# Mamba2 scan feeding a SiLU MLP on one core: how the first unit's C, its decay masks and the opening of the matrix engine are ordered

## The chip, the core and the metric

The kernel runs on one core of a Trainium2 chip. The metric is the device time of one execution in microseconds (us). Seven runs of the kernel before gave a median of 350.6 us, from 350.04 to 353.39.

The core's engines work side by side, each through its own queue of instructions in order: TensorE (PE) multiplies matrices out of SBUF into PSUM, VectorE (DVE), ScalarE (ACT) and GpSimd (POOL) work element by element, SyncE (SP) and ACT issue transfers (DMAs). An instruction that waits holds up all that is queued behind it on its engine.

## What is computed

The input is a state space scan with 4 batches, 8 heads, 768 time steps, 32 channels per head and a state of 16, and an MLP of 256 to 2048 to 256 behind it, all in float32:

```python
L  = exp(cum[:, None] - cum[None, :]) * causal   # decay from step j to step i, in a chunk
y  = ((C @ B.T) * L) @ x  +  (C @ state) * exp(cum)
state = exp(sum(log a)) * state + sum_j decay_from_j * B_j x_j
h  = y_of_all_heads @ w_in
out = (h * sigmoid(h)) @ w_out
```

## The kernel before

The time axis is cut into 12 units of 256 steps (three to a batch), each into four chunks of 64. For a unit, E holds the decays L, G is C times B for each head, M is E times G (written over E), Y the two products that give the scan's output, XM its copy in SBUF. Then come `f_s1` (times w_in, then SiLU) and the product with w_out. Later pairs of units use a seven-product scheme that saves one product in eight; the change does not touch it.

The order of instructions on every engine is written out by hand: the program's order is the engines' order. The text that matters is the opening, until the matrix engine has a backlog of `f_s1` pieces.

**Loads.** SP issues in this order: the first rows of `a` (L192, into `ach`), C of unit 0 in four pieces (`load_t`, L115), `a` again spread over partitions (`pa01`, L200), x of unit 0 (L122), three pieces of w_in (`raw`, L156), B, C and x of unit 1, more weights. ACT issues B of unit 0 (`bn`, L107) and nothing else. `load_unit` calls the same `load_t` for the first unit of each later batch, on SP.

**E of unit 0.** `f_A` (L215) clips the rows of `a`, on DVE. `f_Ab` (L309) spreads them over 128 partitions with one float32 matmul of 512 columns into a PSUM tile `hp` (three buffers), which the machine runs as two passes. `scan_E` (L300, instruction at L304) turns it into E by a scan over 512 columns. There are two such spreads and two scans for a unit, k = 0 and 1.

**C of unit 0.** `f_T(0, 1)` (L347) transposes it on DVE into CT; `f_T2` (L367) makes two masked copies CE on ACT, with `par` (L264) as the mask: two small DVE reductions over `hm`, which POOL makes (L257 to L260).

**B of unit 0.** `f_TP` (L351) transposes it on PE, ACT copies it out (L359), `f_G0` (L406) multiplies it with CE. `f_B` (POOL, L341) multiplies B with the last column of E, and `f_D0` (L391) multiplies that with x; `f_S` (DVE, L430 and L432) makes the chunk states from it, with the decays that `f_P01` (L277, L280) makes from `pa01`. `f_SM` (L440) copies them, `f_M` (L417) makes M, `f_Y` (L460, L469) Y and `f_X` (L482) XM.

**Weights.** Each w_in piece is unpacked on ACT (`w_size`, L164 and L168), DVE (`w_bits`, L176 to L180) and POOL (L184).

**Fillers.** `busy(n, small)` (L223) issues matmuls on zeros: n of 512 bfloat16 columns, then `small` of 64. Their operand `idle` is cleared by a memset (L221) first. Their output goes to the single buffer of `o_ps`.

The part of the order that the change edits, before:

```python
    f_T(0, 1)
    for e in range(2):
        f_T2(0, e)
    f_Ab(0, 0)
    f_Ab(0, 1)
    f_TP(0)
    busy(0, 18)
    f_G0(0)
    busy(2, 10)
    f_Ek(0, 0)
    f_Ek(0, 1)
```

Of the kernel before, what the change touches and what calls it, by code (L numbers as in the profile page):

```python
# [8 lines left out]
FP32 = mybir.dt.float32  # L9
# [3 lines left out]
ALU = mybir.AluOpType  # L13
AX = mybir.AxisListType
# [7 lines left out]
def kernel(  # L22
# [22 lines left out]
    nc = tc.nc  # L45

    batch, H, S, D = x.shape
    N = B.shape[-1]
    Q = 64
# [21 lines left out]
    ps_h = ctx.enter_context(tc.tile_pool(name="ps_h", bufs=3, space=bass.MemoryType.PSUM))  # L71
    ps_o = ctx.enter_context(tc.tile_pool(name="ps_o", bufs=1, space=bass.MemoryType.PSUM))
# [4 lines left out]
    pa, ab, bn, tbc, xt = ({} for _ in range(5))  # L77

    def at(u):
        return u // UPB, u % UPB * UT  # L80

    def load_pa(u, q):

        b, t0 = at(u)
        pa[u] = loads.tile([128, UT], FP32, name="pa")
        q.dma_start(out=pa[u], in_=bass.AP(tensor=a.tensor, offset=a.offset + b * H * S + t0,
                                           ap=[[S, H], [0, N], [1, UT]]))

    def load_ab(u, q):

        b, t0 = at(u)
        ab[u] = loads2.tile([128, 2, H, Q], FP32, name="ab")
        for t in range(4):
            k, c = divmod(t, 2)
            q.dma_start(out=ab[u][64 * c:64 * c + 64, k],
                        in_=bass.AP(tensor=a.tensor, offset=a.offset + b * H * S + t0 + t * Q,
                                    ap=[[0, 64], [S, H], [1, Q]]))

    def load_n(u, i, q):

        b, t0 = at(u)
        if i == 0:
            t = bn[u] = loads.tile([128, 2, H, N], FP32, name="bn")
        else:
            t = tbc[u] = loads.tile([128, 2, 2, 8, N], FP32, name="tbc")[:, 0]
        for k in range(2):
            q.dma_start(out=t[:, k], in_=(B, C)[i][b, :, t0 + 128 * k:t0 + 128 * k + 128].rearrange("h p n -> p h n"))  # L107

    def load_t(u, i, q):

        b, t0 = at(u)
        if u not in tbc:
            tbc[u] = loads.tile([128, 2, 2, 8, N], FP32, name="tbc")
        for g in range(4):
            q.dma_start(out=tbc[u][32 * g:32 * g + 32, i],  # L115
                        in_=(B, C)[i][b, 2 * g:2 * g + 2, t0:t0 + UT].rearrange("e (t r) n -> t e r n", r=8))

    def load_x(u, q):
        b, t0 = at(u)
        xt[u] = loads.tile([128, 2, H, D], FP32, name="xt")  # L120
        for k in range(2):
            q.dma_start(out=xt[u][:, k], in_=x[b, :, t0 + 128 * k:t0 + 128 * k + 128].rearrange("h p d -> p h d"))  # L122

    def load_unit(u):
        load_pa(u, nc.sync)
        if 0 < u < UPB:
            load_n(u, 1, nc.sync)
        else:
            load_t(u, 0, nc.sync)
            load_t(u, 1, nc.sync)  # L130
        load_n(u, 0, nc.sync)
        load_ab(u, nc.sync)
        load_x(u, nc.sync)
# [26 lines left out]
    def w_size(n, what="uv"):  # L160
        if n in raw:
            if "u" in what:
                u = wu[n] = wtp.tile([128, 2, WF], FP32, name="wu")
                nc.scalar.activation(u, raw[n][:, :, :, 1].bitcast(FP32), AF.Abs)  # L164
            if "v" in what:
                v = wv[n] = wtp.tile([128, 2, WF], FP32, name="wv")

                nc.scalar.activation(v, raw[n][:, :, :, 0], AF.Copy, scale=2.0 ** -51, bias=2.0)  # L168
# [20 lines left out]
    A0, A1 = 96, 96 + S // Q  # L189
    early = gpool.tile([128, NF, UT], FP32, name="gT")  # L190
    ach = early[:, 0:2].rearrange("p a (h t) -> p (a h) t", t=Q)
# [3 lines left out]
    QZ = 8 * (Q + 1)  # L195
    pa01 = flat[:, 6 * UT:8 * UT]
    pz01, one01, pfx01 = (flat[:, 8 * UT + QZ * i:8 * UT + QZ * (i + 1)] for i in range(3))
    load_t(0, 1, nc.sync)
    load_n(0, 0, nc.scalar)
    nc.sync.dma_start(out=pa01, in_=bass.AP(tensor=a.tensor, offset=a.offset, ap=[[S, H], [0, N], [1, 2 * UT]]))  # L200
    load_x(0, nc.sync)
# [13 lines left out]
    def f_A():  # L215
        nc.vector.tensor_scalar(out=ach[A0:A1], in0=ach[A0:A1], scalar1=1.0, scalar2=1e-6, op0=ALU.min, op1=ALU.max)
        nc.vector.memset(ach[A0:A1, :, 0:1], 0.0)


    idle = early[:, 4].bitcast(BF16)  # L220
    nc.vector.memset(idle, 0.0)  # L221

    def busy(n, small=0):  # L223
        t = ps_o.tile([128, 512], FP32, name="o_ps")
        for i in range(n):
            nc.tensor.matmul(out=t, lhsT=idle[:, 0:128], rhs=idle, start=True, stop=True)  # L226
        for i in range(small):
            nc.tensor.matmul(out=t[:64, :64], lhsT=idle[:, 0:64], rhs=idle[:, 64:128], start=True, stop=True)  # L228
# [3 lines left out]
    sel = early[:, 2:4].rearrange("p a (s c t) -> p (a s) c t", s=2, c=2)  # L232
# [11 lines left out]
                                fill=1.0, base=-64 * c, channel_multiplier=1)  # L244
    tiny = const.tile([128, 1], FP32, name="tiny")
    nc.scalar.activation(tiny, idle[:, 0:1], AF.Silu)
    busy(5)
    f_A()
    ident = const.tile([128, 128], FP32, name="ident")
    nc.vector.memset(ident, 0.0)  # L250
# [5 lines left out]
    hm = const.tile([128, H], FP32, name="hm")  # L256
# [3 lines left out]
    nc.gpsimd.affine_select(out=hm, in_=hm, pattern=[[N, H]], compare_op=ALU.is_ge,  # L260
                            fill=0.0, base=N - 1, channel_multiplier=-1)
    par = const.tile([128, 2], FP32, name="par")
    for e in range(2):
        nc.vector.tensor_reduce(out=par[:, e:e + 1], in_=hm[:, e::2], op=ALU.add, axis=AX.X)  # L264

    pz = const.tile([128, 4, Q + 1], FP32, name="pz")
    one = const.tile([128, 4, Q + 1], FP32, name="one")
# [32 lines left out]
    def scan_E(u, g0, n, t):  # L300

        if g0 == 0:
            E[u] = sc.tile([128, 2, H, Q], FP32, name="E")
        nc.vector.tensor_tensor_scan(out=E[u].rearrange("p k h t -> p (k h t)")[:, Q * g0:Q * (g0 + n)],  # L304
                                     data0=t.rearrange("p g t -> p (g t)"),
                                     data1=diag[:, 0:n].rearrange("p g t -> p (g t)"),
                                     initial=0.0, op0=ALU.mult, op1=ALU.add)

    def f_Ab(u, k):  # L309

        ab[u, k] = t = ps_h.tile([128, H, Q], FP32, name="hp")
        nc.tensor.matmul(out=t.rearrange("p h t -> p (h t)"),  # L312
                         lhsT=sel[:A1, 2 * u + k].rearrange("r c m -> r (c m)"),
                         rhs=ach[:A1].rearrange("r h t -> r (h t)"), start=True, stop=True)

    def f_Ek(u, k):
        scan_E(u, H * k, H, ab.pop((u, k)))

    def f_E0(u, i, n):

# [23 lines left out]
    def f_T(u, i):  # L344

        t = (BH, CT)[i][u] = sc.tile([128, UT], FP32, name=("bh", "ct")[i])
        nc.vector.transpose(out=t.rearrange("p (t r) -> p r t", r=8), in_=tbc[u][:, i].rearrange("p e r n -> p r e n"))  # L347
        if i == 1:
            tbc.pop(u)

    def f_TP(u):  # L351

        tp = ps_o.tile([128, 512], FP32, name="o_ps")
        for i, t in enumerate((bn[u],) if u == 0 else (bn[u], tbc.pop(u))):
            for k in range(2):
                nc.tensor.transpose(out=tp[:, 256 * i + 128 * k:256 * i + 128 * k + 128],  # L356
                                    in_=t[:, k].rearrange("p h n -> p (h n)"), identity=ident)
        BH[u] = sc.tile([128, UT], FP32, name="bh")
        nc.scalar.activation(BH[u], tp[:, 0:256], AF.Copy)  # L359
        if u > 0:  # L360
            CT[u] = tp[:, 256:512]

    def f_T2(u, e):

        if e == 0:
            CE[u] = sc.tile([128, 2, UT], FP32, name="ce")
        nc.scalar.activation(CE[u][:, e], CT[u], AF.Copy, scale=par[:, e:e + 1])  # L367
# [29 lines left out]
    def f_G0(u):  # L397

        bh, ce = BH.pop(u), CE[u]
        if u not in DP:  # L400
            DP[u] = ps_s.tile([128, 4, 512], FP32, name="gy")
        for k in range(2):
            for c in range(2):
                ts = slice(128 * k + 64 * c, 128 * k + 64 * c + 64)
                for g in range(4):
                    nc.tensor.matmul(out=DP[u][64 * c:64 * c + 64, g, 128 * k:128 * k + 128],  # L406
                                     lhsT=bh[32 * g:32 * g + 32, ts], rhs=ce[32 * g:32 * g + 32, :, ts],
                                     start=True, stop=True, tile_position=(32 * g, 64 * c), skip_group_check=True)
# [401 lines left out]


    f_T(0, 1)
    for e in range(2):
        f_T2(0, e)
    f_Ab(0, 0)
    f_Ab(0, 1)
    f_TP(0)
    busy(0, 18)
    f_G0(0)
    busy(2, 10)  # L820
    f_Ek(0, 0)
    f_Ek(0, 1)
    f_B(0)
    f_D0(0, True)
# [6 lines left out]
    w_size(0)  # L831
    w_bits(0, 2)
    f_Ab(1, 0)
    w_size(1)
    busy(3, 18)
    f_Y(0)

    f_Ek(1, 0)
    f_Ab(1, 1)
    f_X(0)  # L840
    w_size(2)
    w_bits(1, 2)
    load_unit(2)
    f_s1(0, 0)
    f_TP(1)
# [34 lines left out]
    for g, j, todo in steps:  # L880
        f_s1(g, j)
        w_steps(todo)
    load_unit(3)
    late = ("b13 s14", "b14 s15", "b15")

# [122 lines left out]
```

## Time and profile before

| what | value |
|---|---|
| median of seven runs | 350.6 us (350.04 to 353.39) |
| the profiled execution's own time | 350.04 us |
| its span | 348.3 us, so 1.74 us lie around the span |
| TensorE busy | 342.3 us, 98% of the span |
| VectorE, ScalarE, GpSimd busy | 203.9, 162.6, 112.0 us |
| first matmul of `f_s1` | 14.68 us into the span |
| the stretch from which `f_s1` runs without a stop | from 24.50 us |

A row of the timeline gives the start in us from the span's beginning, the duration in us, engine, line, operation, the tile written and the tile read, the shape and the count of like instructions merged into the row; in square brackets stands the idle time before it and what ended that. SPq and ACTq are the issuing of transfers. Busy time of TensorE includes the fillers, so a full row of TensorE says little about the opening. The chain of waits is read backwards from the last instruction: each row is what released the next one.

### The profile page before, as it was taken

The page shows a single profiled execution, that of the slowest core. Times are in us where ns is not written, and L with a number is a line of the kernel's source. Part 1 is how long each engine was busy: PE and PEld are TensorE (multiplying, and loading weights), DVE is VectorE, ACT ScalarE, POOL GpSimd, SP SyncE. Part 2 cuts the span into 40 slices and gives each one's busy share as a digit, 9 for nine tenths or more (in the row PEclk, how much of TensorE's full clock was granted, in tenths as well). Part 3 has the DMA queues.
Part 4 walks back from the last instruction along what each step waited for, and adds up shares of the span by engine and source line. Part 5 has one row for each costly group of instructions (what it writes and reads, how often), then busy time and mean ns, then how long its engine had stood idle before and what let it go on. Part 6 is the DMA issues. An engine that isn't in the chain of part 4 may idle for free.

```text
span 348.3 us, 8381 instructions
## 1 busy us (share of the span) xinstructions
PE 342.3 (98%) x3323; PEld 288.4 (83%) x3324; DVE 203.9 (59%) x406; ACT 162.6 (47%) x399; POOL 112.0 (32%) x140
## 2 busy tenths in 40 slices
PE   8999999999999999999999999999999999999996
PEld 3678888888888888888888888888888888888886
DVE  7998799975795665543763563664652231233912
ACT  3677394323323545455545454644545454454010
POOL 4355345444285122244042244042234112041200
PEclk9999999999999999999999999999999999999999
DMA  6977997699857698857189947057504237512202
GB/s 120 213 216 194 224 334 131 120 210 215 142 111 126 121 187 149 162 107 133 23 166 165 172 91 115 16 102 142 94 2 75 44 56 143 107 24 53 41 7 46
DMA packets 117056, 42.66 MB, mean 122 GB/s; under 512 B 102424, under 2 KB 108824, under 8 KB 117016
## 3 DMA queue, kind: packets, MB, share of 16 engines
q1 hardware_dynamic: 110472, 25.73, 36.2%
q0 software_dynamic: 4464, 16.25, 25.0%
q8 instruction: 26, 0.43, 0.5%
q10 hardware_dynamic: 2080, 0.13, 0.4%
q14 instruction: 14, 0.11, 0.1%
HBM read 22.70 MB, written 3.15 MB: 74 GB/s over the span
## 4 chain that ended last, share of the span: by engine, by line
PE 97%; DVE 1%; ACT 1%; issue 0%; POOL 0%; DVEq 0%; ACTq 0%
PE o_ps L648 36%; PE hp L703 29%; PE hp L505 16%; PE hp L648 3%; PE gy L469 3%; PE gy L460 2%; PE o_ps L611 2%; PE gy L406 2%; PE hp L312 1%; PE gy L391 1%; PE hp L626 1%; PE o_ps L226 1%; PE o_ps L356 0%; PE o_ps L228 0%; DVE E L417 0%
## 5 line engine op out<-in xcount | busy, mean ns | idle before, releaser
L706 DVE TENSOR_TENSOR gT<-hp,p 128x256 f32<-128x256 f32 x64 | 26.8, 419 | 73.6 <-ACT p L717 37.6
L648 PE MATMUL o_ps<-gT,w_out_sb 128*128 128x256 f32 x240 | 60.4, 380 | 0.0
L709 ACT ACTIVATE gT<-gT 128x256 f32<-128x256 f32 x96 | 39.7, 414 | 43.9 <-DVE gT L706 43.9
L505 PE MATMUL hp<-XM,w_in_sb 128*128 128x256 f32 x256 | 59.3, 382 | 0.8 <-ACT XM L482 0.5
L505 PEld LDWEIGHTS hp<-XM,w_in_sb 128*128 128x128 f32 x256 | 48.0, 190 | 8.5 <-POOL w_in_sb L184 1.2
L703 PE MATMUL hp<-raw 128*128 128x256 f32 x192 | 52.7, 380 | 0.0
L558 POOL TENSOR_TENSOR ps<-ps 128x256 f32<-128x256 f32 x35 | 29.5, 843 | 71.2 <-ACT ps L588 69.9
L648 PEld LDWEIGHTS o_ps<-gT,w_out_sb 128*128 128x128 f32 x240 | 45.5, 190 | 6.3
L553 POOL DMA_DIRECT2D gT<-gT x31 | 27.2, 910 | 67.4 <-DVE TN L544 21.5
L703 PEld LDWEIGHTS hp<-raw 128*128 128x128 f32 x192 | 36.2, 190 | 5.4 <-POOL ps L558 0.6
L717 ACT ACTIVATE p<-hp 128x256 f32<-128x256 f32 x64 | 24.5, 383 | 27.4 <-PE hp L703 25.9
L706 DVE TENSOR_TENSOR gT<-hp,u 128x256 f32<-128x256 f32 x32 | 13.6, 424 | 38.6 <-PE hp L703 38.6
L703 PE MATMUL hp<-XM,w_in_sb 128*128 128x256 f32 x128 | 34.1, 389 | 0.0
L507 ACT ACTIVATE gT<-hp 128x512 f32<-128x512 f32 x32 | 18.8, 592 | 25.5 <-PE hp L505 25.5
L703 PEld LDWEIGHTS hp<-XM,w_in_sb 128*128 128x128 f32 x128 | 23.3, 190 | 4.3 <-issue 1.0
L304 DVE TENSOR_TENSOR_SCAN E<-ab,diag 128x256 f32<-128x256 f32 (+1 forms) x32 | 25.1, 825 | 0.8 <-DVE ab L323 0.5
L341 POOL TENSOR_TENSOR BT<-bn,E 128x256 f32<-128x256 f32 x12 | 9.4, 780 | 46.1 <-DVE E L304 38.3
L648 PE MATMUL o_ps<-gT,wu 128*128 128x256 f32 x88 | 22.4, 380 | 0.0
L648 PE MATMUL o_ps<-gT,wv 128*128 128x256 f32 x88 | 22.2, 380 | 0.0
L648 PE MATMUL o_ps<-gT,raw 128*128 128x256 f32 x80 | 20.5, 380 | 0.0
L588 ACT ACTIVATE ps<-o_ps 128x256 f32<-128x256 f32 x35 | 13.3, 382 | 14.8 <-PE o_ps L648 11.8
L703 PE MATMUL hp<-raw,w_in_sb 128*128 128x256 f32 x64 | 19.1, 380 | 0.0
(126 smaller groups left out, 520.4 us busy)
## 6 DMA issues: line engine op xcount, KB each, us to landing
gT<-gT POOLq DMA_DIRECT2D x31, 512.0 KB, 6.1
ab<-in_a_dram SPq DMA_DIRECT2D x40, 128.0 KB
raw<-in_moe_w_in_dram SPq DMA_DIRECT2D x8, 512.0 KB
raw<-in_moe_w_out_dram SPq DMA_DIRECT2D x8, 512.0 KB
xt<-in_x_dram SPq DMA_DIRECT2D x24, 128.0 KB
out_dram<-ot SPq DMA_DIRECT2D x92, 32.0 KB
bn<-in_B_dram SPq DMA_DIRECT2D x22, 64.0 KB
tbc<-in_C_dram SPq DMA_DIRECT2D x40, 32.0 KB
```

Of the source, the lines that this page charges most:

```text
L304: nc.vector.tensor_tensor_scan(out=E[u].rearrange("p k h t -> p (k h t)")[:, Q * g0:Q * (g0 + n)], data0=t.rearrange("p g t -> p (g t)"), ...
L469: nc.tensor.matmul(out=y[32 * q:32 * q + 32, 2 * w + c, 64 * k:64 * k + 64], lhsT=xc[64 * c:64 * c + 64, k, h], rhs=m[64 * c:64 * c + 64, ...
L505: nc.tensor.matmul(out=hp[:, i], lhsT=w_in_sb[:, kc, f * 128:(f + 1) * 128], rhs=xm[:, kc], start=(kc == 0), stop=(kc == KC - 1))
L507: nc.scalar.activation(GTS[g][:, :, j], hp, AF.Silu)
L553: nc.gpsimd.dma_start(out=o[:, js], in_=a[:, js], accum_op=ALU.add)
L558: engine.tensor_tensor(out=o, in0=p, in1=q, op=op)
L588: nc.scalar.activation(p[m].rearrange("p (k c t) -> p c k t", c=2, k=2), o.rearrange("p (c k t) -> p c k t", c=2, k=2), AF.Copy)
L648: nc.tensor.matmul(out=o, lhsT=w(j), rhs=g()[:, j], start=(j == 0), stop=(j == last))
L703: nc.tensor.matmul(out=o, lhsT=w, rhs=x_, start=start, stop=True, skip_group_check=True)
L706: nc.vector.tensor_tensor(out=o, in0=p, in1=q, op=ALU.add)
L709: nc.scalar.activation(o, i, AF.Silu)
L717: nc.scalar.activation(o, i, AF.Copy)
```

## The change

C of unit 0 is loaded on two queues: `load_t` takes two queues and gives its four pieces to them in turn, SP and ACT for unit 0 (SP twice elsewhere). On ACT the two pieces stand ahead of the two of B. DVE transposes C before it makes `par`. The first spread of unit 0 becomes two of 256 columns, each with its own scan; `par` comes behind the first of these scans. The memset of `idle` becomes two, and four matmuls of 128 columns are put ahead of the opening fillers, of which three instead of five are left. The counts of later fillers change.

```diff
-    def load_t(u, i, q):
+    def load_t(u, i, q, q2):
...
-            q.dma_start(out=tbc[u][32 * g:32 * g + 32, i],
+            (q, q2)[g % 2].dma_start(out=tbc[u][32 * g:32 * g + 32, i],
...
-    load_t(0, 1, nc.sync)
+    load_t(0, 1, nc.sync, nc.scalar)
     load_n(0, 0, nc.scalar)
...
-    nc.vector.memset(idle, 0.0)
+    for cs in (slice(0, 128), slice(128, 512)):
+        nc.vector.memset(idle[:, cs], 0.0)
...
-    busy(5)
+    warm = ps_o.tile([128, 512], FP32, name="o_ps")
+    for i in range(4):
+        nc.tensor.matmul(out=warm[:, 0:128], lhsT=idle[:, 0:128], rhs=idle[:, 0:128], start=True, stop=True)
+    busy(3)
     f_A()
...
-    for e in range(2):
-        nc.vector.tensor_reduce(out=par[:, e:e + 1], in_=hm[:, e::2], op=ALU.add, axis=AX.X)
+    def f_par():
+        for e in range(2):
+            nc.vector.tensor_reduce(out=par[:, e:e + 1], in_=hm[:, e::2], op=ALU.add, axis=AX.X)
...
     def f_Ab(u, k):
-        ab[u, k] = t = ps_h.tile([128, H, Q], FP32, name="hp")
-        nc.tensor.matmul(out=t.rearrange("p h t -> p (h t)"),
-                         lhsT=sel[:A1, 2 * u + k].rearrange("r c m -> r (c m)"),
-                         rhs=ach[:A1].rearrange("r h t -> r (h t)"), start=True, stop=True)
-    def f_Ek(u, k):
-        scan_E(u, H * k, H, ab.pop((u, k)))
+        ab[u, k] = []
+        n = H // 2 if u + k == 0 else H
+        for h in range(0, H, n):
+            t = ps_h.tile([128, H, Q], FP32, name="hp")[:, 0:n]
+            ab[u, k].append(t)
+            nc.tensor.matmul(out=t.rearrange("p h t -> p (h t)"),
+                             lhsT=sel[:A1, 2 * u + k].rearrange("r c m -> r (c m)"),
+                             rhs=ach[:A1, h:h + n].rearrange("r h t -> r (h t)"), start=True, stop=True)
+    def f_Ek(u, k, i=0):
+        t = ab[u, k][i]
+        n = t.shape[1]
+        scan_E(u, H * k + n * i, n, t)
...
     f_T(0, 1)
+    f_Ab(0, 0)
+    f_Ek(0, 0)
+    f_par()
     for e in range(2):
         f_T2(0, e)
-    f_Ab(0, 0)
     f_Ab(0, 1)
     f_TP(0)
-    busy(0, 18)
+    busy(0, 14)
     f_G0(0)
-    busy(2, 10)
-    f_Ek(0, 0)
+    busy(2)
+    f_Ek(0, 0, 1)
     f_Ek(0, 1)
...
-    busy(3, 18)
+    busy(3, 28)
     f_Y(0)
```

More of the change, by code (lines that the diff above doesn't have):

```diff
@@ L128, in load_unit @@
         else:
-            load_t(u, 0, nc.sync)
-            load_t(u, 1, nc.sync)
+            load_t(u, 0, nc.sync, nc.sync)
+            load_t(u, 1, nc.sync, nc.sync)
         load_n(u, 0, nc.sync)
```

## The prediction

> **What bounds the kernel now.** I read the page's first and fourth part, then the chain of waits, then the opening's timeline engine by engine.
>
> ```profile
> PE 342.3 (98%) x3323; PEld 288.4 (83%) x3324; DVE 203.9 (59%) x406; ACT 162.6 (47%) x399; POOL 112.0 (32%) x140
> ...
> PE 97%; DVE 1%; ACT 1%; issue 0%; POOL 0%; DVEq 0%; ACTq 0%
> ```
>
> TensorE sets the time, but until 24.50 us much of its work is filler. The change touches the opening alone, so its whole worth is how far it moves this last row of the chain, behind which `f_s1` runs without a stop:
>
> ```profile
> 3.57 2.80 PE hp L312 x4
> ...
> 9.38 0.42 PE hp L391 x32
> 9.80 0.02 issue
> 9.83 0.23 DVE st L430
> ...
> 24.50 12.35 PE hp L505 x56
> ```
>
> The chain passes through the spreads (L312), then `f_D0` (L391), then the states (L430). VectorE's timeline shows who stands beside it:
>
> ```profile
> 3.56 0.43 DVE L255 COPY diag<-gT 128x512 f32<-128x512 f32 x1
> 4.75 0.22 DVE L264 TENSOR_REDUCE par<-hm 128x1 f32<-128x4 f32 x2 [0.76 <-POOL hm L260]
> 4.93 0.64 DVE L347 STREAM_TRANSPOSE ct<-tbc 128x256 f32<-128x256 f32 x1
> 5.50 2.34 DVE L304 TENSOR_TENSOR_SCAN E<-hp,diag 128x512 f32<-128x512 f32 x2
> 7.76 0.40 DVE L277 TENSOR_SCALAR gT<-gT 128x512 f32<-128x512 f32 x1
> 8.19 1.56 DVE L280 TENSOR_TENSOR_SCAN gT<-gT 128x520 f32<-128x520 f32 x1
> ```
>
> VectorE stands still 0.76 us for the mask `hm`; from 4.75 on it has work without a gap over 0.15 us until past 22.4 us, when M of unit 1 ends. What moves VectorE's queue at 9.8 us moves the 24.50, if nothing else is late.
>
> **Part 1: C on two queues, ahead of B.** The four issues of C take SP 1.74 us (1.29 to 3.03). Two go to ACT, so the last starts at 1.72 instead of 2.6. In the landing records C's pieces arrive at 3.45, 3.88, 4.26 and 4.45: 1.85 us after the start of the last issue, at most 2.16 for the first. So the last now lands at 3.6 to 3.9 (an estimate from these rows). VectorE is free at 3.99 (3.56 + 0.43): C is no longer late for it, and even landing at 4.45 it would cost little, as part 3 shows.
>
> ACT issues 0.85 us more ahead of its table load (1.92 to 3.20, then 2.75 to 4.03) and `tiny`; its next work is CE, not before 5.5: hidden, with 1.3 us of cover. B of unit 0 is issued 0.85 us later; before it landed at 3.21 and 4.09, and its first reader is TensorE at 6.21: hidden, about 1.2 us left.
>
> SP comes 0.87 us earlier (two issues of 0.43) to `pa01`, x, w_in and unit 1's loads. This matters, since their landings stand close to their readers: `pa01` lands at 7.61 and is read at 7.76; the second w_in piece lands at 12.79 and ACT reads it at 12.81 after 0.23 us of waiting; C of unit 1 lands at 16.87 and TensorE reads it at 16.92. All three must come earlier for a gain to pass. The DMA row is at 0.04 of its 16 engines from 4.0 to 4.5 us and at 0.39 to 0.52 until 5.5, so there is room for 0.87 us of earlier work; bounds are 0 (B's small packets take all the room) and 0.87. I take 0.5 or more, enough for what follows.
>
> The Trainium skill, DMA: Bandwidth & Descriptors, section "Issuing engines are not separate DMA queues", speaks against this part: queues on several engines share the same 16 DMA engines and save only the issue time. By it the part would be worth the issue time of two pieces at most, and that is also what I counted; the DMA engines were idle at 4.0 to 4.5 here, so the rule takes nothing more away.
>
> **Part 2: the opening fillers.** A memset of 64 words takes 0.11 us (L238) and the whole one 0.27 (L221), so the first filler starts about 0.16 us earlier, at 1.10. The second memset adds some 0.07 us on VectorE, inside the 0.21 us that `f_A` waits for `a` at 2.72. The old fillers start 0.427 us apart (records of L226), so four of 128 columns take about 0.43 in all (a quarter of a filler each, an estimate). `busy(3)` writes the one `o_ps` buffer and waits for the last of the four: a gap of about 0.25 us; behind it are only fillers and the spreads. Three fillers then end near 3.04 in the stream, and the spreads can't start before `f_A`'s memset at 3.21 + 0.07, so as before at 3.42. A new gap of about 0.35 us, free in itself; what it may do to the clock is a rival below.
>
> **Part 3: the chain through E.** The four passes of L312 start at 3.42, 4.41, 5.26 and 5.78 and last 1.19, 1.06, 0.68 and 0.59: the first two run at half the pace of the last. Halves of 256 columns at the slow pace start at 3.42, 3.98, 4.41 and 4.83 (0.427 each, 0.13 more for the first), so the first half's sum is complete at about 4.61 and the second's at 5.47. The second spread is the same work behind the same work: complete at 6.37, as before.
> VectorE now: C transposed 4.0 to 4.64; scan of the first half 4.65 to 5.3 (0.67 for 128x256 from other units' rows at L304; from PSUM at least half of 1.21); `par` to 5.45; second half 5.50 to 6.12; then it would be ready at 6.1 for the second scan, which waits for the spread's 6.37 and starts at 6.41. Before it started at 6.64. **Gain 0.23 us**; the other 0.3 us that VectorE wins are lost to a new wait for TensorE. CE starts at 5.5 instead of 5.6 and still ends before ACT copies B out at 6.62: nothing.
>
> **Part 4: `f_D0` ahead of the states.** It ends at 9.80 and L430 starts at 9.83, 0.08 us behind the end of the scan before it (8.19 + 1.56 = 9.75), while neighbours on VectorE start about 0.07 us before their forerunner ends (5.50 against 4.93 + 0.64 = 5.57). So L430 loses 0.15 us to `f_D0`, which is late through the ten small fillers (8.88 to 9.38): POOL's product is ready at 7.93 + 0.73 = 8.66 and x at 8.57. Now 4 and 10 small ones go, `f_D0` follows at about 8.7 and ends near 9.15, long before the scan. I take **0.12 us** of 0 to 0.15.
>
> **Part 5: ten more small fillers before `f_Y(0)`.** Eighteen take 0.76 us (11.40 to 12.16); 28 about 0.32 more. With `f_D0` 0.6 us earlier they end near 11.9; `f_Y(0)` is wanted at 12.42 - 0.35 = 12.07. Free, with a cover of 0.15; without it up to 0.32 us.
>
> **Sum.** 0.23 + 0.12 = 0.35 us. Behind it I followed each handover: weights unpacking, E and states of unit 1 are VectorE's own queue; XM of unit 0 on ACT needs the earlier second w_in piece; `f_s1(0, 1)` at 17.37 needs the earlier C of unit 1 (its other wait, POOL's 17.33, moves along). After 24.50 the weights lead `f_s1` by over 0.7 us. So 350.04 - 0.35 = 349.7 against the profiled execution. That one is the fastest of the seven; against their median the same step is 350.6 - 0.35 = **350.2 us**, and this I predict. 0.35 us is 0.1% of the time; about 0.5% (1.75 us) is what a measurement of this kernel can tell from no change.
>
> **Rivals.**
> *The clock opens sooner (0.2).* If TensorE's slow pace ends a few tenths sooner, the second spread isn't late and VectorE goes through: 6.64 - 6.10 = 0.54, with part 4's 0.15 near 0.7. Time 350.6 - 0.7 = 349.9; on the profiled execution 349.3. For it: the fillers begin 0.16 us sooner. Against: the gaps of part 2.
> *Given back to a transfer (0.15).* If `pa01`, the second w_in piece and C of unit 1 land when they did, `f_s1(0, 1)` starts at 17.28 and the gain is at most 0.1: 350.5. For it: they land 0.02 to 0.15 us before their readers. Against: the idle DMA engines at 4.0 to 4.5.
> *Slower: the clock opens late (0.12).* The slow pace ended in the third pass: 0.517 us from start to start, between 0.853 slow and 0.427 fast, puts it at 5.44, 4.2 us after the first filler. If the two gaps (0.6 us of 2.3) put that off past the second spread, its passes take 0.853 and 1.06 from 5.26: complete at 7.17, the scan at 7.21, 0.57 later than before; 350.6 + 0.57 = 351.2. It decides from an opening later than about 5.9. If the slow pace lasts through `f_Y(0)` (1.37 us fast) as well, up to another 1.4: 352.6. Against: the gap of 0.47 us at 6.6 to 7.06 did not bring the slow pace back.
> The Trainium skill, TensorE: Matmul & The Clock Gate, Part 1, has the gate open after a busy window of about 3.4 us that runs free of the kernel's start, and bids to keep it filled; this speaks against the gaps. The 4.2 us of this trace fit one such window, which by the page would be re-drawn in every execution: the gain would then scatter between nothing and the first rival's.
>
> **Chances.** Forecast 0.53, the rivals 0.2, 0.15, 0.12. Faster by over 0.5% needs 348.85 or less: no case reaches it, 0.04 for what I don't see. Slower by over 0.5%: the worse end of the third rival, 0.07. Within: 0.89. Range 349.3 (the first rival on the profiled execution) to 351.2 (the third).
>
> **What would show it.** C transposed at 4.0, ahead of `par`; the second 512-column scan of unit 0 starting at 6.4 with an idle time before it that TensorE ends (at 6.1 without one: first rival; at 7.2: third); L430 straight behind its forerunner near 9.4; the long row of L505 from about 24.15 us. If that row starts there and the time does not fall, the main stretch has changed and my reading of it is wrong. If L430 is early and the row is not, look for ACT waiting on w_in near 12.5 and TensorE on C near 16.9.

## The result and the profile after

The changed kernel takes 352.96 us (median of 20 runs, 351.00 to 353.94), the kernel before 350.92 us (47 runs): a ratio of 1.0058, 95% interval 1.0045 to 1.0070. It is 2.0 us slower. I had forecast 0.35 us faster and gave a range up to 351.2.

The profiled execution took 353.07 us, 3.03 more than that of before. The page's first and fourth part, after:

```profile
PE 344.6 (98%) x3323; PEld 290.1 (83%) x3324; DVE 204.9 (58%) x408; ACT 163.2 (46%) x399; POOL 112.6 (32%) x140
...
PE 92%; DMA 3%; SPq 3%; ACTq 0%; DVE 0%; issue 0%; POOL 0%; ACT 0%
```

Transfers, absent from the chain of before, hold 3% of it now. The chain of waits, after, shows the first of them and where the long row of `f_s1` (L520 here) starts:

```profile
2.20 5.74 DMA bn<-in_B_dram
...
27.10 0.39 ACT XM L497
27.50 0.04 issue
27.54 12.35 PE hp L520 x56
```

Not every row of this chain is what held up the next. Between the two parts shown it goes through a w_in piece that lands at 21.97, ahead of VectorE's L180 at 22.02; but L180 follows L178 on VectorE without a gap (21.35 + 0.75 = 22.10), as it did before (18.32 + 0.75 = 19.07, L180 at 18.99). What was lost is read from the engines' own rows below.

The long row starts at 27.54 instead of 24.51 (by its single records), 3.03 us later, which is the whole difference: 353.07 - 27.54 and 350.04 - 24.51 are both 325.53. What lies behind the opening takes as long as before. In every run below the time is 325.5 to 325.8 us more than this start, so the start can be read in place of the time.

What VectorE does in the opening, after (the timeline):

```profile
3.77 0.63 DVE L362 STREAM_TRANSPOSE ct<-tbc 128x256 f32<-128x256 f32 x1
4.52 0.69 DVE L312 TENSOR_TENSOR_SCAN E<-hp,diag 128x256 f32<-128x256 f32 x1
5.13 0.20 DVE L271 TENSOR_REDUCE par<-hm 128x1 f32<-128x4 f32 x2
5.37 0.69 DVE L312 TENSOR_TENSOR_SCAN E<-hp,diag 128x256 f32<-128x256 f32 x1
7.08 1.22 DVE L312 TENSOR_TENSOR_SCAN E<-hp,diag 128x512 f32<-128x512 f32 x1 [1.02 <-PE hp L325]
8.22 0.40 DVE L285 TENSOR_SCALAR gT<-gT 128x512 f32<-128x512 f32 x1
8.65 1.56 DVE L288 TENSOR_TENSOR_SCAN gT<-gT 128x520 f32<-128x520 f32 x1
12.54 0.22 DVE L445 COPY st<-hp 128x64 f32<-128x64 f32 x1 [2.33 <-PE hp L406]
```

The first four rows are as forecast, even a little sooner. Then VectorE waits twice for TensorE: 1.02 us for the second spread, 2.33 us for the chunk sums (`f_D0`, L406 here). TensorE's own timeline before (rows from B's transposes to the chunk sums), and after:

```profile
6.21 0.38 PE L356 MATMUL o_ps<-ident,bn 128*128 128x128 f32 x2
7.06 0.73 PE L228 MATMUL o_ps<-gT 128*64 128x64 bf16 x18 [0.47 <-ACT bh L359]
7.72 0.69 PE L406 MATMUL gy<-ce,bh 32*64 32x128 f32 x32
9.31 0.45 PE L391 MATMUL hp<-xt,BT 64*32 64x64 f32 x32
```

```profile
3.29 3.75 PE L325 MATMUL hp<-gT 108*128 108x256 f32 x6
6.83 0.42 PE L371 MATMUL o_ps<-ident,bn 128*128 128x128 f32 x1
7.98 0.47 PE L371 MATMUL o_ps<-ident,bn 128*128 128x128 f32 x1 [0.72 <-DMA bn<-in_B_dram]
8.93 0.91 PE L229 MATMUL o_ps<-gT 128*64 128x64 bf16 x14 [0.47 <-ACT bh L374]
9.77 1.16 PE L421 MATMUL gy<-ce,bh 32*64 32x128 f32 x32
10.86 0.61 PE L227 MATMUL o_ps<-gT 128*128 128x512 bf16 x1
11.82 0.68 PE L406 MATMUL hp<-xt,BT 64*32 64x64 f32 x32 [0.36 <-issue]
```

The loss has three parts in these rows. B's second half is not there until 7.94 (landing records; 4.09 before), so its transpose ends at 8.46 instead of 6.59: 1.87 us. Not all of that is the wait: the transpose of the first half, which was there, already starts at 6.83 instead of 6.21, behind spreads that ran at the slow pace to their end. With B in time at the same pace both transposes end at 7.54 (a run below), so about 1 us of the 1.87 is the wait for B. All that follows is at the slow pace too, G at 1.16 us instead of 0.69; from that transpose's end to the end of `f_D0` it is 4.04 us instead of 3.17: 0.87. From there to the long row it is 15.04 instead of 14.75: 0.29, in which the 28 small fillers hold `f_Y(0)` until 15.54, 0.55 us behind the end of M (14.99), where before it followed after 0.15. Sum: 1.87 + 0.87 + 0.29 = 3.03.

### The profile page after: what moved, and what is told of

The parts are those of the page before. It is cut to its first block, busy times and chain, and to the rows that moved or that the text cites. A ratio compares the mean times of both kernels' runs of the same rounds, so it can differ in the third digit from the quotient of the medians.

```text
span 351.4 us, 8383 instructions
## 1 busy us (share of the span) xinstructions
PE 344.6 (98%) x3323; PEld 290.1 (83%) x3324; DVE 204.9 (58%) x408; ACT 163.2 (46%) x399; POOL 112.6 (32%) x140
## 4 chain that ended last, share of the span: by engine, by line
PE 92%; DMA 3%; SPq 3%; ACTq 0%; DVE 0%; issue 0%; POOL 0%; ACT 0%
PE o_ps L663 36%; PE hp L718 28%; PE hp L520 15%; PE hp L663 3%; PE gy L484 2%; PE o_ps L626 2%; SPq L107 2%; PE gy L475 2%; PE gy L421 2%; DMA bn<-in_B_dram 2%; DMA raw<-in_moe_w_in_dram 1%; PE gy L406 1%; PE hp L641 1%; SPq L156 0%; SPq L122 0%; ACTq L115 0%
## 5 line engine op out<-in xcount | busy, mean ns | idle before, releaser
L520 PE MATMUL hp<-XM,w_in_sb 128*128 128x256 f32 x256 | 59.3, 381 | 0.9 <-ACT XM L497 0.5
L520 PEld LDWEIGHTS hp<-XM,w_in_sb 128*128 128x128 f32 x256 | 48.1, 190 | 8.7 <-POOL w_in_sb L184 1.2
```

The lines of the kernel that those rows point to most:

```text
L520: nc.tensor.matmul(out=hp[:, i], lhsT=w_in_sb[:, kc, f * 128:(f + 1) * 128], rhs=xm[:, kc], start=(kc == 0), stop=(kc == KC - 1))
```

## The experiments

Theory: **B is late**, because two pieces of C stand ahead of it on ACT's queue and SP's next loads now run beside it. Rival: **the slow pace lasts**, because of the new gaps between the opening fillers. "Above" and "below" are against the kernel before on the same chip, by medians; the interval is the ratio's.

**C on SP again** (one line of the change undone).

```diff
-    load_t(0, 1, nc.sync, nc.scalar)
+    load_t(0, 1, nc.sync, nc.sync)
```

> The changed kernel with one thing undone: all four pieces of C go on SP again, so ACT issues B first, as before. Everything else of the change stays. Theory (B is late): the second half of B lands near 4.1 us instead of 7.9, TensorE transposes B near 6.6 instead of 8.0, the long row of f_s1 comes back by about 2.5 to 3 us, and the time is within 0.6 us of the kernel before on the same chip (a ratio of 0.999 to 1.002). Rival (the clock opens late because of the new gaps in the fillers): the slow pace still holds through the spreads and beyond, and the time stays 1 to 2 us above the kernel before (ratio 1.003 to 1.006).

Ratio 1.0027 (1.0007 to 1.0048), 0.8 us above. B's last packet moves at 3.98 us (it lands at 4.33), and its transpose starts at 6.97 straight behind the spreads; but the row starts at 25.76, 1.8 us sooner than with the change and not 2.5 to 3. The spreads are at the slow pace to their end, and in this execution x of unit 1 lands at 20.73, for which TensorE waits 0.7 us. So B is over half of the loss, and something else is left.

**The split alone**, in the kernel before.

```diff
-    load_t(0, 1, nc.sync)
+    load_t(0, 1, nc.sync, nc.scalar)
```

> The kernel before with only the load of C split over SP and ACT, ahead of B. Fillers, spreads, order of VectorE all as before. Theory (B is late): B's second half lands near 8 us, TensorE waits for it until 8.0 and stands still for about 1.5 us behind the spreads; 1.3 to 2.5 us slower than before (ratio 1.004 to 1.007). Rival (the clock and the fillers): no change, within 0.4 us.

Ratio 1.0033 (1.0018 to 1.0049), 0.8 us above, its fastest run at 351.43. B's second half lands at 7.69, its transpose starts at 7.73. The rival is out for this part: the split costs by itself, though less than the 1.3 to 2.5 us that I expected.

**The fillers of before** in the changed kernel: one memset, `busy(5)`, `busy(0, 18)`, `busy(2, 10)`, `busy(3, 18)`.

> The changed kernel with the fillers of before: one memset, five long ones at the opening, 18 small ones, two long and ten small, three long and 18 small. Theory (B is late): B still lands near 8 us and most of the loss stays, 1.2 to 2.2 us above the kernel before; the clock may open before the spreads end, as it did before, but closes or not in the wait for B. Rival (the clock): the slow pace ends near 5.4 us and the loss is gone, within 0.4 us of the kernel before or faster.

Ratio 1.0064 (1.0042 to 1.0086), four runs, 2.3 us above. B lands at 7.94 and the loss stays, although the opening has no new gap. The fillers alone are not the cause. In three of the four runs the mean granted clock is 0.995 or 0.99; the last part comes back to this.

**The decays behind B on ACT**, off SP.

```diff
-    nc.sync.dma_start(out=pa01, ...)
+    nc.scalar.dma_start(out=pa01, ...)
```

> The changed kernel with the 256 KB load of the decays (pa01) on ACT's queue behind B instead of on SP's ahead of x. B is issued as late as in the changed kernel, but no 2 KB packets of another queue stand beside it. If B is late because its 64 B packets take turns with the 2 KB packets on eight DMA engines: it lands near 5.0 to 5.8 us, TensorE transposes it straight behind the spreads near 7, and the time is 0 to 1 us above the kernel before. If B is late only because it is issued 0.9 us later or because x takes the room: it lands near 7 to 8 us as in the changed kernel, and the time stays 1.5 to 2.5 us above. pa01 itself should land near 7.5 to 8.5, which may hold VectorE up by some tenths.

Ratio 1.0017 (0.9998 to 1.0036). B is issued as late as in the changed kernel and lands at 5.29 instead of 7.94. TensorE's timeline of this run has the two transposes together, without a wait:

```profile
3.36 3.75 PE L325 MATMUL hp<-gT 108*128 108x256 f32 x6 [0.20 <-DVE gT L217]
6.90 0.64 PE L371 MATMUL o_ps<-ident,bn 128*128 128x128 f32 x2
8.01 0.91 PE L229 MATMUL o_ps<-gT 128*64 128x64 bf16 x14 [0.47 <-ACT bh L374]
8.85 1.16 PE L421 MATMUL gy<-ce,bh 32*64 32x128 f32 x32
```

So it is `pa01` beside B that makes B late; being issued 0.9 us later costs 1.2 us of landing, the neighbour another 2.65. But G still takes 1.16 us without a late B: the slow pace is a loss of its own, and this execution took 352.57 while others of the same kernel took 350.8.

**The kernel before again**, for a second profile.

> The kernel before, unchanged, for a second profile of it. If the end of TensorE's slow pace is drawn anew in every execution, this profile shows it at another time than 5.44 us (somewhere between 5 and 8.5), the second scan of unit 0 starts between 6.6 and 7.2 and the time moves with it by up to 0.6 us; if it is fixed by the kernel, it shows 5.4 again. The ratio is 1 within its interval.

Ratio 0.9988 (0.9959 to 1.0017). The slow pace ends near 4.2 us here and near 5.4 in the first profile of the same kernel. The second scan starts at 6.42 without any change to the kernel, sooner than the 6.6 I had set as its earliest; that is what I had forecast the change to gain. Yet the row starts at 24.52, as before. Two waits of this run, which the kernel before's first profile has not, say why (13.4 to 24.6 us):

```profile
PEld hp L391 <- DMA xt<-in_x_dram: 0.2, 1, 0.2
DVE st L432 <- PE hp L391: 0.2, 1, 0.2
```

TensorE waits for x of unit 1, whose last part lands at 19.50, and VectorE for TensorE's product with it: the state step L432 starts at 19.92, as before at 19.93, though all ahead of it on VectorE was 0.3 us sooner (L180 at 18.69 instead of 18.99). The 0.2 us won in the opening are given back to a transfer. The chain of this run names another, the fifth piece of w_in, which lands at 23.35 ahead of ACT's unpacking; but XM starts at 24.09, 0.04 us behind the end of Y as before, so that piece held nothing up.

**The new fillers alone**, in the kernel before.

> The kernel before with the new fillers alone (two memsets, four short and three long ones at the opening, 14, two, three and 28). Theory (the change loses by the late B; fillers add a little): 0 to 0.3 us slower, through the 28 small ones if they run past the end of M. Rival (the gaps in the opening fillers put off the end of the slow pace): 0.5 to 1 us slower, with the slow pace in the profile until 7 us or later.

Ratio 1.0010 (0.9982 to 1.0037): the median is 0.1 us above, but the runs fall in two groups, seven from 350.2 to 351.2 and five from 352.1 to 353.1 us. The profiled one is of the second, at 352.57. Its groups of TensorE from 1 to 14 us (count, busy us, mean ns):

```profile
L316 PE MATMUL hp<-gT 108*128 108x512 f32 x6 | 5.7, 1092 | 0.1
L410 PE MATMUL gy<-ce,bh 32*64 32x128 f32 x32 | 1.2, 430 | 0.0
```

and the same of the kernel before:

```profile
L312 PE MATMUL hp<-gT 108*128 108x512 f32 x7 | 4.8, 788 | 0.0
L406 PE MATMUL gy<-ce,bh 32*64 32x128 f32 x32 | 0.7, 280 | 0.0
```

Spreads at 1.09 us a pass and G at 430 ns a matmul are the slow pace. It lasts until about 13 us here (a spread's pass at 12.44 still takes 0.95 us), and costs about 2 us (352.57 against 350.62, the first group's median). Both sides of what I expected were wrong in form: not a shift of the median but a second group.

**E in quarters alone** (C transposed first, masks behind, C on SP, fillers of before).

> The kernel before with E begun in quarters, C transposed ahead of the masks and the masks behind the first quarter; C on SP and the fillers of before. By the third step of the prediction: 0.2 us faster where TensorE's slow pace ends near 5.4 us, nothing where it lasts past the spreads, so 0 to 0.25 us faster in the median. If splitting the spread costs something of its own, up to 0.3 us slower.

Ratio 0.9993 (0.9967 to 1.0019). Row from 24.67. No gain can be told from none.

**The same with early chunk sums**: `busy(2)` for `busy(2, 10)`.

> As the run with E in quarters alone, with the ten small fillers behind the two long ones taken away as well, so that the chunk sums (f_D0) come early. By the fourth step of the prediction 0.1 us faster than that run, 0.2 to 0.35 us faster than the kernel before in the median; the first state copy starts straight behind the scan of the decays. If f_D0 wasn't what the states waited for, no different from that run.

Ratio 0.9994 (0.9983 to 1.0005). The first state copy starts at 9.60 instead of 9.98, as the fourth step said. The row starts at 24.66 instead of 24.67. The chain of this run:

```profile
14.98 4.66 DMA xt<-in_x_dram
19.68 0.35 PE hp L402 x16
...
24.66 1.35 PE hp L516 x5
```

X of unit 1 lands at 19.64 and takes the place of the wait that went.

**New fillers without gaps.** The four short ones and four long ones write one tile:

```diff
-    busy(3)
+    for i in range(4):
+        nc.tensor.matmul(out=warm, lhsT=idle[:, 0:128], rhs=idle, start=True, stop=True)
```

> As the run with the new fillers alone, but the opening ones follow each other without a gap: the four short ones and four long ones write one and the same tile, so no filler waits for another, and the fourth long one fills the time to the spreads. 14, two, three and 28 stay. If the two opening gaps put off the end of TensorE's slow pace (five of twelve executions of the new fillers alone lay at 352 us and more): those are gone or rare, one in ten as in the kernel before, and the median lies within 0.3 us of it. If the thinner fillers behind the spreads are the cause: again about four in ten executions near 352 to 353.

Ratio 1.0003 (0.9988 to 1.0018); one of twelve runs at 352 us or more, 350.83 in the median. By the rows' starts, at 0.427 a filler, 0.27 us are still empty between the last filler and the spreads here, against 0.26 and 0.32 us in the two gaps of the new fillers; "without gaps" means this opening from here on.

**One filler less** in the kernel before: `busy(4)` for `busy(5)`.

> The kernel before with four instead of five long fillers at the opening, which leaves one gap of about 0.43 us ahead of the spreads and changes nothing else. If an opening gap alone puts off the end of the slow pace: in a share of the executions (three in ten or more) the time is 1.5 to 2.5 us higher. If it takes the thinner fillers behind the spreads as well: the same times as the kernel before.

Ratio 1.0022 (1.0001 to 1.0044); seven of twelve runs at 352 us or more (six without one at 355.91), three of 29 of the kernel before on this chip. One gap of 0.37 us ahead of the spreads is enough, where 0.27 us in the run before was not. Together the two runs show that the gaps are the cause of the second group, not the thinner fillers behind the spreads. How long a gap may be is not settled by them.

**B first on ACT**, then the two pieces of C (E in quarters, fillers of before).

```diff
+    load_n(0, 0, nc.scalar)
     load_t(0, 1, nc.sync, nc.scalar)
-    load_n(0, 0, nc.scalar)
```

> E in quarters and the fillers of before, with C on two queues, but on ACT the two pieces of B stand ahead of the two of C. If the place of B behind C is what costs: B lands near 4.1 us as before, C near 4.0 to 4.6, and the time is that of the run with E in quarters alone (350.3 to 350.9). If it is the second queue as such (SP's next loads starting 0.9 us earlier, beside B): B lands later than 5 us and the time is 0.8 us or more above the kernel before.

Ratio 1.0091 (1.0065 to 1.0117), the slowest of all. Now C is late. VectorE's timeline of this run:

```profile
6.94 0.64 DVE L358 STREAM_TRANSPOSE ct<-tbc 128x256 f32<-128x256 f32 x1 [3.08 <-DMA tbc<-in_C_dram]
7.43 0.63 DVE L308 TENSOR_TENSOR_SCAN E<-hp,diag 128x256 f32<-128x256 f32 x1
```

ACT's last piece of C was issued at about 2.5 us and landed at 6.86. So it is not B's place alone: here, too, the load that stands last on ACT beside SP's `pa01` is late. TensorE stands still from 6.19 to 9.36 us in this run, and what it does next is at the slow pace again (the last part has the clock).

**What the runs pointed to, put together**: C on SP, E in quarters, early chunk sums, early and gapless opening.

> What the other runs point to put together: C on SP and B first on ACT as before, E in quarters, ten small fillers fewer ahead of the chunk sums, and an opening of fillers that starts 0.16 us sooner and has no gap. If the slow pace ends sooner and in nearly every execution: 0.2 to 0.7 us faster than the kernel before (ratio 0.998 to 0.9995), with few executions above 351. If the opening makes no difference: as the run with E in quarters and early chunk sums, ratio 0.9994.

Ratio 0.9997 (0.9981 to 1.0013). Its profile has the earliest row of all, 24.24 us, and 349.82 us; over twelve runs no gain can be told.

**The change without gaps**, then also **with the decays behind B** (the two edits above, on the changed kernel).

> The changed kernel with a gapless opening (four short and four long fillers on one tile), all else as changed. If late B and gaps are two causes that add: B still lands near 7.9 us, the slow pace ends before the wait for B in most executions, and the time is 0.8 to 1.5 us above the kernel before instead of 2.0. If the wait for B (TensorE standing still at 7 to 8 us) keeps the slow pace by itself, gaps or not: 1.7 to 2.5 us above. If the gaps were all of it: within 0.4 us.

> The same with the decays' load (pa01) behind B on ACT's queue, so that nothing of 2 KB stands beside B. If the two causes are the whole loss: B lands near 5.3 us, and the time is within 0.3 us of the kernel before, on either side, with one execution in ten at 352 us or more. If something else of the change costs: 0.5 us or more above the kernel before.

The first: ratio 1.0048 (1.0027 to 1.0069), 1.2 us above; B at 7.83, row from 25.71. The second: 1.0008 (0.9997 to 1.0018), none of eleven runs at 352 us or more; B at 5.14. With both away the loss is gone, and no gain appears. VectorE's timeline of the second:

```profile
6.55 1.23 DVE L313 TENSOR_TENSOR_SCAN E<-hp,diag 128x512 f32<-128x512 f32 x1 [0.35 <-PE hp L326]
8.79 0.43 DVE L286 TENSOR_SCALAR gT<-gT 128x512 f32<-128x512 f32 x1 [1.01 <-DMA gT<-in_a_dram]
```

The decays, now last on ACT, land at 8.77 and VectorE waits 1.01 us for them.

**X before the decays on SP**, gapless, B behind C on ACT.

> The changed kernel with the gapless opening and, on SP, x of unit 0 ahead of the decays (pa01). If B's lateness came from the 2 KB packets beside it: B lands near 5.3 us. If pa01 then lands by 7.6 us, VectorE goes on without a wait, the state copy starts near 9.5 and the time is 0.2 to 0.5 us below the kernel before; if pa01 lands near 8.8 as in the run with it behind B, the time is that run's, within 0.3 us of the kernel before. If the early C and the quarters gain nothing of themselves: the same as the kernel before even with pa01 in time.

Ratio 1.0029 (1.0017 to 1.0041), 0.8 us above. B lands at 5.98, but the decays, now behind x, at 9.55, later than I had allowed for in either case; VectorE waits 1.24 us. Another load is late in B's place; what held it was not tested.

## Why the prediction was wrong

**The step that failed: part 1, "B of unit 0 is issued 0.85 us later ... hidden, about 1.2 us left".** I moved B's landing by its issue alone. It moved from 4.09 to 7.94: by 1.2 us in the run that kept `pa01` away from it (5.29) and by 2.65 more with it. I had the idle DMA engines at 4.0 to 4.5 us as room for SP's loads, and did not ask what those loads would meet: the stretch was idle because B was through before `pa01` came. In the changed kernel's records B's second half reaches its semaphore in two halves, eight arrivals from 4.66 to 5.39 and eight from 7.69 to 7.94; `pa01`'s load also shows eight arrivals. From 5.0 to 7.0 us only some 220 packets of 64 B move, against over 700 in the half microsecond from 2.0 in the kernel before. The Trainium skill, DMA: Bandwidth & Descriptors, section "Queues, rings and completion order", says that a DMA engine goes round its queues a packet at a time; the two halves fit that, if `pa01` lies on eight of the sixteen engines. I had cited another section of that page and found that it took nothing away; this one bears on it and I left it out. The size: without gaps the changed kernel is still 1.2 us above by medians (1.7 by the ratio), of 2.0.

A late B may also cost more than its wait, and part 1 had nothing for either. The runs' mean granted clock is 0.995 or 0.99 in three of four with the fillers of before, in three of seven without gaps and in one of seven with the split alone, and these are the slowest of theirs; with B in time and no gaps none of eleven is under 0.998. The run with B first has 0.99, and its trace shows what that is: the clock granted falls to 0.5 at 8.15 us, with TensorE still since 6.19, and is back at 14.98. So in part of the executions the wait for B seems to bring the slow pace back. That is argued from these figures; no execution of those three kernels with such a clock was profiled.

**Part 2, "a new gap of about 0.35 us, free in itself".** The second gap came as forecast (the last filler starts at 2.53, so at 0.427 a filler TensorE is empty from about 2.96 to 3.29), but it is not free: the run with one gap in the kernel before shows it, and the new fillers without gaps, which lose nothing. This was the third rival. Its mechanism was right; its chance of 0.12 was too small (five of twelve runs with these fillers alone), and its price of 0.57 to 2 was nearer its upper end. I took its evidence against, that the gap of 0.47 us at 6.6 to 7.06 did no harm, from a place where the pace was already fast. The Trainium skill (TensorE: Matmul & The Clock Gate, Part 1), which I had quoted against the change, lets the pace turn after a busy window of about 3.4 us that does not begin with the kernel. That the end is drawn anew agrees with these runs: it lies at 4.2 and 5.4 us in two profiles of one kernel, and near 13 in some with gaps. A full window of work ahead of it is not what all of them show: from the first filler to the end it is 4.2 us in one of the two profiles and 3.0 in the other.

**Part 3, E's chain.** C landed at 3.49, was transposed from 3.77, and the quarters ran at 4.52 and 5.37: right. The wait for the second spread was forecast, at 6.41; it was 7.08 after, and 6.55 in the run with both losses away. The gain did not follow, since the kernel before also starts that scan at 6.42 when the pace turns early.

**Part 4, the chunk sums.** Right in the run made for it (9.60 against 9.98), and without worth: x of unit 1 was late next. I had named `pa01`, the second w_in piece and C of unit 1 as the transfers to watch, and missed x of unit 1. The second rival, that the gain is given back to a transfer, is what the runs without the two losses show: to x of unit 1 with C on SP, to `pa01` with it last on ACT.

**Part 5.** The cover of 0.15 us was gone because `f_D0` came late: the 28 small fillers cost 0.4 us in the profile after.

What stays open: how the 2.0 us divide between the gaps and the late B. Without the new gaps the kernel is 1.2 us above instead of 2.0, but the two intervals (1.0045 to 1.0070 and 1.0027 to 1.0069) overlap, and with the fillers of before, which have no such gap either, it is 2.3 us above in four runs. Whether `pa01` truly lies on eight engines is argued from the arrivals, not shown. A run with the decays on a third queue, or in smaller packets, was not tried.

## What to carry to other kernels

A load that is put on a second queue, or behind others there, must be followed through what the first queue will now issue beside it: count the packets of both, not the issue time. In an opening that transfers fill to the end, each order makes another load the late one, and a chain shortened on the engines gains nothing until the transfers behind it are sooner too. Fillers that open the matrix engine should follow each other and the first real work as closely as they can, and a kernel whose start depends on that is judged by many executions, not by one profile. A row of the chain of waits is believed when the engine's own row shows the idle time for it.

## What the runs showed of the hardware

- TensorE's slow pace (a pass of 512 float32 columns every 0.853 us instead of 0.427) ended between 4.2 and 7.9 us, or near 13, in kernels that differ only in this opening; one gap of 0.37 us ahead of the spreads put seven of twelve executions about 2 us behind. The page's clock does not show this opening: it reads 1.0 from the start. In the trace the records of the granted clock begin where the durations change: at 5.43 and 4.22 us in the kernel before, at 13.27 in the changed one.
- The pace can be lost again: with B first on ACT it was fast from 4.74 us, TensorE then stood still from 6.19 to 9.36, the granted clock was 0.5 from 8.15 to 14.98, and G took the 1.16 us of the slow pace. So the fast pace was gone 1.96 us after TensorE's last work.
- 128 KB of 64 B packets landed within 3.3 us of their first issue with no packet over 512 B beside them (0.80 to 4.09), and in 6.2 us (1.72 to 7.94) beside 2 KB packets of another queue.
- The last sixteenth of a load can come long after the rest: of the second half of x of unit 1, 15 arrivals were there by 18.23 us and the last came at 19.64 in the run with early chunk sums (18.26 and 19.05 in the kernel before).
